# Attention and feed-forward on one core: the first batch's last four down-projection blocks in three rounded passes

## The chip, the cores and the metric

One core of a Trainium2 chip runs the whole program. The metric is the device time of one execution in microseconds (us); lower is better. TensorE (PE) multiplies matrices, and PEld in the profile is its weight load. VectorE (DVE) and ScalarE (ACT) do the elementwise work, GpSimd (POOL) helps them, and SyncE (SP) issues most transfers.

## What is computed

```
# q, k, v: [8 batches, 8 heads, 576, 64];  p: [8, 8, 32, 64];  float32
packed = softmax(p k^T / 8) v                 # per head, 32 rows
attn   = softmax(q packed^T / 8) packed       # per head, 576 rows
x = attn as [8*576, 512]
h = x @ w_in                                  # 512 -> 2048
g = h * tanh(softplus(h))                     # "mish"
out = g @ w_out                               # 2048 -> 512
```

The two weights arrive as 64-bit floats and are turned into float32 on the chip.

## The kernel before

**Work and steps.** The eight batches follow each other, and each has 16 blocks of 128 hidden columns, so there are 128 blocks, and a loop over `t` (L1043) takes one block per step; `f` is the block within its batch. In a step PE does the up-projection of block `t` (`up`, L795: 12 matmuls into two PSUM tiles `ps_h`), ACT applies mish (`mish`, L824) and PE does the down-projection of an earlier block (`down`, L857: four chunks of 128 rows, into four accumulators `acc`). Up to step 16 the block that is brought down is the one of the step before; later it is the one two steps back. The order of a step on PE is: down chunks 0 and 1, up, chunks 2 and 3, with other work let in between.

**Two ways to multiply.** A full float32 matmul appears in the trace as two PE instructions. The other way splits both operands into a rounded high part and a remainder and does three matmuls, high by high, high by remainder and remainder by high (`down_one`, L841). The up-projection does this from block 4 on, the down-projection from batch 1 on. The down-projection of all 16 blocks of batch 0 uses full float32 (L863). For the three passes the weight `wo[f]` is split by `split_wo` (L111: ACT writes `wo_hi`, DVE writes `wo_lo`), which stands in steps 16 to 31, and the activations `g` are split by `halves` (L833).

**Weights of the first batch.** While batch 0 runs, 32 pieces of weight are fetched into eight staging slots `w_st` and decoded: `words` (L685) is two ACT instructions (the second writes `wround`) and two on POOL (the second writes `wsign`), and `join` (L698) is two on DVE for each piece, one with `wsign`, one with `wround`. At odd `f`, `packed_half` (L743) makes the next two blocks' up weights: 16 matmuls on PE into two tiles `ps_w`, then ACT writes `wp_hi` and DVE writes `wp_lo`. The tiles `ps_w`, `ps_a` (turned weights), `ps_pp` (values), `ps_ppT` and `ps_s` (scores) all share one pool of two PSUM buffers, so a tile waits until the one two places before it has been read.

**The next batch's attention.** The attention of batch 1 is a generator (`attention`, L581) that is moved on by one piece at each `advance(gen)` (L907, which first emits what is in `pending`). In steps with even `f` there are three such places, at odd `f` ("chunk" steps) one.

**What sets the order.** PE follows program order throughout. Up to step 16 (`by_hand`) so do DVE, ACT, POOL and SP: each engine takes its instructions in the order in which the code emits them. After that a scheduler orders all engines but PE.

**Memory.** The staging pool `stg` is closed at step 14, and a pool `late` takes its place, with room for the split parts of the first eight weights, three pairs of split activations `g_hi`, `g_lo`, and one pair `r_hi`, `r_lo` for the left-over rows.

Of the kernel before, what the change touches and what calls it, by code (L numbers as in the profile page):

```python
# [17 lines left out]
GB = 3  # L18
# [13 lines left out]
HALFWAY = 8  # L32
SPLIT0 = 14
# [10 lines left out]
def body(  # L44
# [57 lines left out]
    stage = ExitStack()  # L102
    stg = stage.enter_context(tc.tile_pool(name="stg", bufs=STB, side="right"))
    late = []
# [3 lines left out]
    def wo_slot(dtype, name):  # L108
        return wts.tile([P, DO], dtype, name=name, tag="wo", bufs=NF + 1)

    def split_wo(i):  # L111
        if i < HALFWAY:
            wo_hi[i], wo_lo[i] = [late[0].tile([P, DO], F32R, name=f"wo_{x}{i}") for x in ("hi", "lo")]
        else:
            wo_hi[i], wo_lo[i] = wo_slot(F32R, "wo_hi"), wo_slot(F32R, "wo_lo")
        both = [
            nc.scalar.copy(out=wo_hi[i], in_=wo[i]),
            nc.vector.tensor_tensor(out=wo_lo[i], in0=wo[i], in1=wo_hi[i].bitcast(F32), op=ALU.subtract),
        ]
        for x in both:  # L120
            tc.keep_in_program_order(x)
# [255 lines left out]
    class Later(Batch):  # L377
# [203 lines left out]
        def attention(self):  # L581
# [88 lines left out]
    class Weight:  # L670
# [6 lines left out]
        def fetch(self):  # L677
            self.st = stg.tile([P, 2 * FC], I32, name="w_st")
            nc.sync.dma_start(
                out=self.st.rearrange("p (m x) -> p m x", m=2),  # L680
                in_=w_in_v[:, 2 * self.g:2 * self.g + 2, self.n * FC:(self.n + 1) * FC],
            )
            self.dst = wi[self.n // 2][self.g][:, self.n % 2].rearrange("p m x -> p (m x)")

        def words(self):  # L685
            x = self.st.rearrange("p (n t) -> p n t", t=2)
# [20 lines left out]
    class WeightOut(Weight):  # L707
# [3 lines left out]
        def fetch(self):  # L711
            self.st = stg.tile([P, 2 * FC], I32, name="w_st")
            nc.sync.dma_start(out=self.st, in_=w_out_v[:, self.i, :])
            self.dst = wo[self.i] = wo_slot(F32, "wo32")
# [53 lines left out]

    def split_tiles(name="g", bufs=GB):
        return [late[0].tile([P, MAIN], F32R, name=f"{name}_{n}", bufs=bufs) for n in ("hi", "lo")]  # L770

    def split(*srcs):

        hi, lo = split_tiles("r", 1)
# [6 lines left out]
    class Group:  # L781
# [75 lines left out]
    def down(grp, c):  # L857
# [4 lines left out]
        if b == 0:  # L862
# [13 lines left out]
    def down_rest(grp):  # L876
# [6 lines left out]
        if i == 0:  # L883
            rest["o"] = late[0].tile([P, DO], F32, name="o_rest", bufs=1)
# [81 lines left out]
    def fetch(n):  # L966
        for x in pieces[done["fetch"]:n]:
            x.fetch()
# [17 lines left out]
    with tc.manual_schedule(engines={mybir.EngineType.PE}):  # L986
# [56 lines left out]
        for t in range(n_groups + LAG):  # L1043
# [32 lines left out]
            if t == SPLIT0:  # L1076
                stage.close()
                late.append(ctx.enter_context(tc.tile_pool(name="late", bufs=1, side="right", reuse_waits="tile")))
            if 0 <= t - NF < NF:
                split_wo(t - NF)  # L1080
# [43 lines left out]
            if chunk and t > 1:  # L1124
# [28 lines left out]
            if grp:  # L1153
                grp.halves()
                if t <= 13 and t != 1:
                    words(2 * t + 9)
# [6 lines left out]
            if dn and not away:  # L1163
                down(dn, 3)
            if grp and f % 4 == 2 and (b or f == NF - 2):
# [8 lines left out]
            elif b == 0 and not chunk:  # L1174
# [30 lines left out]
```

## Time and profile before

| | us |
|---|---|
| median of 3 runs | 729.82 (729.26 to 731.15) |
| the profiled execution's own time | 729.15 |
| its span, first to last instruction | 726.9 |
| PE busy | 716.2 (99%) |
| DVE / ACT / POOL busy | 430.4 / 315.6 / 70.8 |

The span is what the engines' records cover; 2.25 us of the execution's own time lie around it. "Busy" is an average over stages, so what an engine has to spare is to be read stage by stage. The chain of waits follows the work that ended last back from the end; a stretch in which it runs through PE alone is one in which PE sets the time.

### The profile page before, as it was taken

To read this page: it belongs to the slowest core of one execution; us is meant where nothing else is said; L and a number is where in the kernel's file an instruction comes from. 1 tells how busy PE (TensorE), PEld (TensorE's weight loads), DVE (VectorE), ACT (ScalarE), POOL (GpSimd) and SP (SyncE) were. 2 spreads that over 40 slices of the span, in tenths; PEclk is the share of its full clock that TensorE was granted. 3 is DMA by queue.
4 is the path that set the end of the run, shared out by engine and by line. 5 is a ranking of instruction groups with operands and counts; after the bars stand their busy time and mean duration, and the time that the engine had idled before them with its cause. 6 is when DMAs were issued, how large, how long until landed. Compare 5 with 4: busy or idle time off the path is not lost.

```text
span 726.9 us, 12741 instructions
## 1 busy us (share of the span) xinstructions
PE 716.2 (99%) x5094; PEld 554.9 (76%) x5094; DVE 430.4 (59%) x763; ACT 315.6 (43%) x710; POOL 70.8 (10%) x103
## 2 busy tenths in 40 slices
PE   8899999999999999999999999999999999999997
PEld 5455555788887788787887888887888878888885
DVE  4999878847746466545645566465574566443322
ACT  4876646545533344344342444253442524433221
POOL 0585540000000000000000000000000000000000
PEclk9999999999999999999999999999999999999999
DMA  9999971642203612145102442144101000010002
GB/s 237 303 298 226 311 122 31 130 78 67 33 29 73 110 34 33 66 67 99 18 15 81 67 98 34 44 72 74 33 1 59 15 1 1 1 59 1 1 0 73
DMA packets 187114, 56.34 MB, mean 78 GB/s; under 512 B 175024, under 2 KB 177328, under 8 KB 187056
## 3 DMA queue, kind: packets, MB, share of 16 engines
q1 hardware_dynamic: 183376, 47.14, 29.3%
q0 software_dynamic: 1344, 4.20, 1.5%
q10 hardware_dynamic: 2336, 4.20, 1.5%
q8 instruction: 40, 0.66, 0.4%
q14 instruction: 18, 0.15, 0.1%
HBM read 46.07 MB, written 9.44 MB: 76 GB/s over the span
## 4 chain that ended last, share of the span: by engine, by line
PE 93%; DVE 4%; DMA 1%; SPq 0%; issue 0%; ACT 0%; DVEq 0%
PE ps_h L805 27%; PE acc L843 15%; PE acc L845 14%; PE acc L844 14%; PE acc L863 6%; PE ps_w L719 4%; PE ps_rest L843 2%; PE ps_rest L845 2%; PE ps_rest L844 2%; PE ps_h L467 2%; DMA q_t<-in_q_dram 1%; PE ps_h L540 1%; PE ps_s L467 1%; PE ps_a L520 1%; DVE wi L705 1%; DVE wi L700 1%
## 5 line engine op out<-in xcount | busy, mean ns | idle before, releaser
L827 ACT ACTIVATE g<-ps_h 128x256 f32<-128x256 f32 (+2 forms) x256 | 97.9, 385 | 262.9 <-PE ps_h L805 239.0
L843 PE MATMUL acc<-wo_hi,g_hi 128*128 128x512 f32 x448 | 179.6, 401 | 0.0
L844 PE MATMUL acc<-wo_lo,g_hi 128*128 128x512 f32 x448 | 176.7, 394 | 0.0
L845 PE MATMUL acc<-wo_hi,g_lo 128*128 128x512 f32 x448 | 176.6, 394 | 0.0
L805 PE MATMUL ps_h<-aT_hi,wp_hi 128*128 128x256 f32 x496 | 153.0, 308 | 0.0
L805 PE MATMUL ps_h<-aT_lo,wp_hi 128*128 128x256 f32 x496 | 146.4, 295 | 0.2 <-DVE aT_lo L344 0.2
L805 PE MATMUL ps_h<-aT_hi,wp_lo 128*128 128x256 f32 x496 | 146.2, 295 | 0.0
L838 DVE CAST g_hi<-g 128x512 fp32r<-128x512 f32 x112 | 47.4, 424 | 165.9 <-ACT g L827 165.9
L843 PEld LDWEIGHTS acc<-wo_hi,g_hi 128*128 128x128 f32 x448 | 84.2, 188 | 32.3 <-issue 14.7
L805 PEld LDWEIGHTS ps_h<-aT_hi,wp_hi 128*128 128x128 f32 x496 | 93.4, 188 | 15.2 <-issue 5.9
L805 PEld LDWEIGHTS ps_h<-aT_lo,wp_hi 128*128 128x128 f32 x496 | 93.4, 188 | 12.5 <-issue 3.3
L845 PEld LDWEIGHTS acc<-wo_hi,g_lo 128*128 128x128 f32 x448 | 84.1, 188 | 19.8
L805 PEld LDWEIGHTS ps_h<-aT_hi,wp_lo 128*128 128x128 f32 x496 | 93.4, 188 | 0.0
L844 PEld LDWEIGHTS acc<-wo_lo,g_hi 128*128 128x128 f32 x448 | 84.1, 188 | 9.2
L839 DVE TENSOR_TENSOR g_lo<-g,g_hi 128x512 fp32r<-128x512 f32 x112 | 77.0, 687 | 6.8 <-DVE g_hi L838 0.5
L863 PE MATMUL acc<-wo,g 128*128 128x512 f32 x128 | 61.3, 604 | 0.0
L730 ACT CAST wp_hi<-ps_w 128x512 fp32r<-128x512 f32 x56 | 30.1, 591 | 65.5 <-PE ps_w L719 65.5
L731 DVE TENSOR_TENSOR wp_lo<-ps_w,wp_hi 128x512 fp32r<-128x512 f32 x56 | 35.9, 683 | 9.1 <-ACT wp_hi L730 9.1
L863 PEld LDWEIGHTS acc<-wo,g 128*128 128x128 f32 x128 | 22.4, 189 | 22.7 <-issue 19.2
L872 POOL DMA_DIRECT2D out_dram<-o x16 | 9.0, 561 | 311.2 <-DVE o L852 307.1
L719 PE MATMUL ps_w<-wi,ppT 64*32 64x512 f32 (+1 forms) x576 | 36.8, 548 | 1.9 <-DVE wi L705 1.3
L311 DVE TENSOR_REDUCE sm<-a 128x18 f32<-128x576 f32 (+1 forms) x15 | 11.9, 792 | 28.4 <-ACT a L306 28.4
(135 smaller groups left out, 792.3 us busy)
## 6 DMA issues: line engine op xcount, KB each, us to landing
w_st<-in_moe_w_in_dram SPq DMA_DIRECT2D x16, 512.0 KB, 7.6
w_st<-in_moe_w_out_dram SPq DMA_DIRECT2D x16, 512.0 KB, 7.3
q_n<-in_q_dram SPq DMA_DIRECT2D x56, 144.0 KB, 3.2
v_n<-in_v_dram SPq DMA_DIRECT2D x56, 128.0 KB, 2.8
k_n<-in_k_dram SPq DMA_DIRECT2D x32, 144.0 KB, 3.3
out_dram<-o ACTq DMA_DIRECT2D x14, 256.0 KB, 2.0
k_n<-in_k_dram SPq DMA_DIRECT2D x96, 32.0 KB, 2.0
out_dram<-o POOLq DMA_DIRECT2D x12, 256.0 KB, 2.6
```

The lines of the kernel that those rows point to most:

```text
L467: nc.tensor.matmul(out=ps[u][h * NP:(h + 1) * NP, :], lhsT=packT[u * D:(u + 1) * D, n:n + NP], rhs=xT[u * D:(u + 1) * D, h ^ g, :], start= ...
L719: nc.tensor.matmul(out=ps[h * NP:(h + 1) * NP, :], lhsT=ppTb[row:row + D, g, h * NP:(h + 1) * NP], rhs=w[row:row + D], start=True, stop=Tr ...
L730: nc.scalar.copy(out=hi, in_=ps)
L731: nc.vector.tensor_tensor(out=lo, in0=ps, in1=hi.bitcast(F32), op=ALU.subtract)
L805: nc.tensor.matmul(out=ps, lhsT=w[:, fs], rhs=a[:, g, cs], start=(n == 0), stop=(n == 5))
L827: nc.scalar.activation(out=self.act[:, a:a + m], in_=ps[:, :m], func=AF.Mish)
L838: nc.vector.tensor_copy(out=hi, in_=self.act)
L839: nc.vector.tensor_tensor(out=lo, in0=self.act, in1=hi.bitcast(F32), op=ALU.subtract)
L843: nc.tensor.matmul(out=acc, lhsT=hi[:, cs], rhs=wh, start=start, stop=False)
L844: nc.tensor.matmul(out=acc, lhsT=hi[:, cs], rhs=wl, start=False, stop=False)
L845: nc.tensor.matmul(out=acc, lhsT=lo[:, cs], rhs=wh, start=False, stop=stop)
L863: nc.tensor.matmul(out=accs[c], lhsT=grp.act[:, cs], rhs=wo[f], start=f == 0, stop=f == NF - 1)
```

## The change

- In batch 0, blocks 12 to 15 (`THREE = 12`) are brought down in three rounded passes. `halves` for these blocks (ACT copies the high part, DVE subtracts) comes right after the block's up-projection, and `split_wo` of weights 12 to 15 moves to the ends of steps 11 to 14. In steps 28 to 31 nothing is split any more.
- The staging pool stays open to the end. Its slots hold, once a weight piece is decoded, the split weights 12 to 15 and 0 to 3 and the split activations of blocks 12 to 15; the tiles `wround` and `wsign` (four buffers each) hold the later blocks' `g_hi`, `g_lo` and the left-over rows' `r_hi`, `r_lo`, which had three and one.
- Decoding runs one or two pieces earlier from step 9 on.
- The attention of batch 1 gets a second and third place to move on in odd steps from `f` = 7 (`not chunk or f >= 7`), the maximum of its second softmax is taken for each half on its own, and the division goes from DVE to POOL.

```diff
+THREE = 12
+FIRST_SLOTS = 2
...
     def split_wo(i):
-        if i < HALFWAY:
-            wo_hi[i], wo_lo[i] = [late[0].tile([P, DO], F32R, name=f"wo_{x}{i}") for x in ("hi", "lo")]
+        own = STB - (NF - THREE)
+        if i >= THREE or i < own:
+            pair = slot(F32R, "wo_pair", KEPT <= i < own)
+            wo_hi[i], wo_lo[i] = pair[:, 0], pair[:, 1]
         else:
-            wo_hi[i], wo_lo[i] = wo_slot(F32R, "wo_hi"), wo_slot(F32R, "wo_lo")
+            late = i < own + (NF - THREE) // 2
+            wo_hi[i], wo_lo[i] = wo_slot(F32R, "wo_hi", late), wo_slot(F32R, "wo_lo", late)
...
                 flush()
+                self.peak(slice(g, g + 1))
                 yield
             both = slice(0, 2)
-            self.peak(both)
-            yield
             self.rise(both)
             yield
-            self.share(both)
+            yield
+            self.tally(both)
+            for u in range(2):
+                self.divide(both, u, nc.gpsimd)
+            yield
+            yield
...
         def halves(self):
             if self.b == 0:
-                return
-            self.g = split_tiles()
-            hi, lo = self.g
-            nc.vector.tensor_copy(out=hi, in_=self.act)
+                if self.f < THREE:
+                    return
+                pair = slot(F32R, "g_pair", True)
+                hi, lo = self.g = pair[:, 0], pair[:, 1]
+                nc.scalar.copy(out=hi, in_=self.act)
+            else:
+                hi, lo = self.g = split_tiles()
+                nc.vector.tensor_copy(out=hi, in_=self.act)
             nc.vector.tensor_tensor(out=lo, in0=self.act, in1=hi.bitcast(F32), op=ALU.subtract)
...
-        if b == 0:
+        if b == 0 and f < THREE:
             nc.tensor.matmul(out=accs[c], lhsT=grp.act[:, cs], rhs=wo[f], start=f == 0, stop=f == NF - 1)
...
-            if 0 <= t - NF < NF:
+            if 0 <= t - NF < THREE:
                 split_wo(t - NF)
...
             if t <= 13:
-                join(2 * t + 5 + t // 12 - (t == 9))
+                join(2 * t + 5 + 2 * (t > 9))
...
                 grp.up(0)
                 grp.up(1)
+                if t < NF:
+                    grp.halves()
...
                     if t == 9:
-                        join(2 * t + 5)
+                        join(2 * t + 7)
...
-                    words(2 * t + 9)
+                    words(2 * t + 9 + 2 * (t > 8))
...
+            if THREE <= t + 1 < NF:
+                split_wo(t + 1)
...
-            elif b == 0 and not chunk:
+            elif b == 0 and (not chunk or f >= 7):
                 advance(gen)
```

**PE, steps 7 and 8.** `ps_w` are the up weights made in step 7, `acc` are down chunks, and `ps_a` are the turned attention weights of batch 1. Before:

```order
L719 MATMUL ps_w_919<-wi_1_97,ppT 32x256
L863 MATMUL acc_549<-wo_561,g 128x512
L863 MATMUL acc_550<-wo_561,g 128x512
L863 MATMUL acc_547<-wo_641,g 128x512
L520 MATMUL ps_a_954<-ident,a_693 128x128 x4
L863 MATMUL acc_548<-wo_641,g 128x512
```

Now:

```order
L881 MATMUL acc_549<-wo_561,g 128x512
L881 MATMUL acc_550<-wo_561,g 128x512
L527 MATMUL ps_a_951<-ident,a_693 128x128 x4
L881 MATMUL acc_547<-wo_641,g 128x512
L527 MATMUL ps_a_960<-ident,a_693 128x128 x4
L881 MATMUL acc_548<-wo_641,g 128x512
```

The first `ps_a` stands two down chunks behind `ps_w` where it stood three behind.

**PE, steps 9 and 10.** `ps_pp` is one half of the values' product, `ps_ppT` turns both normalized halves, and `ps_s` are the second scores. Before (12 `up` rows stand where the dots are):

```order
L863 MATMUL acc_549<-wo_644,g 128x512
L556 MATMUL ps_pp<-v_n,a1T_n 32x64 x20
L863 MATMUL acc_550<-wo_644,g 128x512
L863 MATMUL acc_547<-wo_780,g 128x512
L556 MATMUL ps_pp<-v_n,a1T_n 32x64 x20
L863 MATMUL acc_548<-wo_780,g 128x512
...
L863 MATMUL acc_549<-wo_780,g 128x512
L567 MATMUL ps_ppT<-ident,pp 128x128 x2
```

Now:

```order
L881 MATMUL acc_549<-wo_644,g 128x512
L563 MATMUL ps_pp<-v_n,a1T_n 32x64 x20
L881 MATMUL acc_550<-wo_644,g 128x512
L574 MATMUL ps_ppT<-ident,pp 128x128 x2
L881 MATMUL acc_547<-wo_780,g 128x512
L474 MATMUL ps_s_1143<-xT,ppT 32x288 x4
L474 MATMUL ps_s_1144<-xT,ppT 32x288 x4
```

Between the second `ps_pp` and `ps_ppT` there is one down chunk now; there were two chunks and an up-projection. On DVE the same place reads, now:

```order
L763 TENSOR_TENSOR wp_lo<-ps_w_1062,wp_hi 128x256
L763 TENSOR_TENSOR wp_lo<-ps_w_1063,wp_hi 128x256
L711 SCALAR_TENSOR_TENSOR wi_0_98<-wi_0_98,wsign 128x512
L711 SCALAR_TENSOR_TENSOR wi_1_99<-wi_1_99,wsign 128x512
L716 ISA wi_0_98<-wi_0_98,wround 128x1024
L716 ISA wi_1_99<-wi_1_99,wround 128x1024
L276 TENSOR_SCALAR pp<-ps_pp,rs 128x128
L575 COPY ppT<-ps_ppT 128x128 x2
```

The four join rows of a pair of pieces stand between `wp_lo` of step 9 and the normalization `pp` that `ps_ppT` reads, as they did before.

**ACT, steps 11 to 12.** `wo_pair` is the split weight 12, `a_1142` the second softmax of batch 1, `g` the mish of block 12 and `g_pair` its split. Now:

```order
L762 CAST wp_hi<-ps_w_1227 128x256
L699 ACTIVATE wo_1084<-w_st 128x512
L700 ACTIVATE wround<-w_st 128x512
L123 CAST wo_pair<-wo_901 128x512
L313 ACT_TABLE_LOAD
L313 ACTIVATE a_1142<-a_1142 128x1152
L841 ACT_TABLE_LOAD
L841 ACTIVATE g<-ps_h_90 128x256
L841 ACTIVATE g<-ps_h_91 128x256
L843 ACTIVATE g_rest_1268<-ps_h_91 128x64
L853 CAST g_pair<-g 128x512
```

Before, the exponential stood one round of `wp_hi` later, in step 13, and no split followed the mish:

```order
L751 CAST wp_hi<-ps_w_1327 128x256
L306 ACT_TABLE_LOAD
L306 ACTIVATE a_1160<-a_1160 128x1152
L777 CAST r_hi<-g_rest_462 128x4x64
L827 ACT_TABLE_LOAD
L827 ACTIVATE g<-ps_h_90 128x256
```

## Rows read from the trace of the kernel before

**Rows 1.** Windows: length; busy PE, PEld, DVE, ACT, POOL; granted clock; DMA share; GB/s.

```profile
100.00:110.00 10.00, 10.00 (x69) 5.74 (x68) 9.42 (x13) 4.15 (x12) 4.78 (x7) 1.00 0.92 163
200.00:300.00 100.00, 100.00 (x713) 82.82 (x712) 55.38 (x100) 39.49 (x91) 2.82 (x6) 1.00 0.26 54
```

**Rows 2.** Chain of waits, steps 7 to 9: start, length, engine, tile, line, count.

```profile
71.91 2.77 PE acc L863 x6
74.68 0.55 PE ps_a L520 x4
...
83.37 0.59 PE ps_w L719 x16
83.96 1.05 PE acc L863 x2
85.02 0.83 PE ps_pp L556 x40
```

**Rows 3.** Chain of waits, steps 12 to 14.

```profile
103.99 3.43 PE acc L863 x8
107.42 1.59 PE ps_h L805 x12
109.01 0.59 PE ps_w L719 x16
109.61 3.63 PE acc L863 x8
...
114.83 1.72 PE acc L863 x4
```

**Rows 4.** Timeline of PE, batch 1: first of six rounded passes, and what follows them.

```profile
140.18 0.40 PE L843 MATMUL acc<-wo_hi,g_hi 128*128 128x512 f32 x1
...
141.57 0.28 PE L805 MATMUL ps_h<-aT_hi,wp_hi 128*128 128x256 f32 x1
```

**Rows 5.** Timeline of the weight loads, step 8; in brackets idle time and releaser.

```profile
74.57 0.42 PEld L520 LDWEIGHTS ps_a<-ident,a 128*128 128x128 f32 x4 [0.72 <-DVE wp_lo L752]
```

**Rows 6.** Timeline of DVE, steps 5, 9 and 10.

```profile
62.40 1.28 DVE L700 SCALAR_TENSOR_TENSOR wi<-wi,wsign 128x512 int32<-128x512 int32 x2
63.60 1.29 DVE L705 CUSTOM_DVE_ANT_0 wi<-wi,wround 128x1024 uint16<-128x1024 uint16 x2
...
84.46 0.75 DVE L752 TENSOR_TENSOR wp_lo<-ps_w,wp_hi 128x256 fp32r<-128x256 f32 x2 [1.33 <-ACT wp_hi L751]
...
87.01 1.85 DVE L700 SCALAR_TENSOR_TENSOR wi<-wi,wsign 128x512 int32<-128x512 int32 x2
88.78 1.69 DVE L705 CUSTOM_DVE_ANT_0 wi<-wi,wround 128x1024 uint16<-128x1024 uint16 x2
90.39 0.34 DVE L269 TENSOR_SCALAR pp<-ps_pp,rs 128x128 f32<-128x128 f32 x1
```

**Rows 7.** One kind of join instruction: least, median, greatest ns, and when.

```profile
L705 DVE CUSTOM_DVE_ANT_0 wi<-wi,wround x16: 677/880/1098, 19.9 to 102.9; 128x1024 uint16<-128x1024 uint16 x16
```

**Rows 8.** Timeline of ACT, steps 12, 13 and 16.

```profile
104.41 0.67 ACT L688 ACTIVATE wo<-w_st 128x512 f32<-128x512 f32 x1
104.97 0.68 ACT L689 ACTIVATE wround<-w_st 128x512 int32<-128x512 uint32 x1
...
110.36 1.28 ACT L306 ACT_TABLE_LOAD   x1
111.65 1.16 ACT L306 ACTIVATE a<-a 128x1152 f32<-128x1152 f32 x1
...
121.26 0.67 ACT L827 ACTIVATE g<-ps_h 128x256 f32<-128x256 f32 x2
...
121.90 0.65 ACT L117 CAST wo_hi<-wo 128x512 fp32r<-128x512 f32 x1
```

**Rows 9.** Timeline of DVE, steps 16 and 17.

```profile
122.58 0.69 DVE L118 TENSOR_TENSOR wo_lo<-wo,wo_hi 128x512 fp32r<-128x512 f32 x1 [0.18 <-ACT wo_hi L117]
...
127.09 0.69 DVE L839 TENSOR_TENSOR g_lo<-g,g_hi 128x512 fp32r<-128x512 f32 x1
127.85 0.69 DVE L852 COPY o<-acc 128x512 f32<-128x512 f32 x1
```

More of the change, by code (lines that the diff above doesn't have):

```diff
@@ L17 @@
 LAG = 2
-GB = 3
 KVB = 8
@@ L101, in body, with slot, wo_slot @@
     wi = [[const.tile([P, 2, 2, QC], F32, name=f"wi{c}_{g}") for g in range(2)] for c in range(DF // FC)]
[L102 to L104 removed]
+    stg = ctx.enter_context(tc.tile_pool(name="stg", bufs=1, side="right"))
+    KEPT = STB - FIRST_SLOTS - (NF - THREE)
     wo, wo_hi, wo_lo = {}, {}, {}
[L108 to L109 removed]
+    def slot(dtype, name, first):
+        tag, n = ("st_a", FIRST_SLOTS) if first else ("st_b", STB - FIRST_SLOTS)
+        return stg.tile([P, 2, FC], dtype, name=name, tag=tag, bufs=n)
+    def wo_slot(dtype, name, late):
+        tag, n = ("wo_b", NF - THREE) if late else ("wo_a", THREE + 1)
+        return wts.tile([P, DO], dtype, name=name, tag=tag, bufs=n)
     def split_wo(i):
[L112 to L115 removed]
+        own = STB - (NF - THREE)
+        if i >= THREE or i < own:
+            pair = slot(F32R, "wo_pair", KEPT <= i < own)
+            wo_hi[i], wo_lo[i] = pair[:, 0], pair[:, 1]
+        else:
+            late = i < own + (NF - THREE) // 2
+            wo_hi[i], wo_lo[i] = wo_slot(F32R, "wo_hi", late), wo_slot(F32R, "wo_lo", late)
         both = [
@@ L119, in split_wo @@
         ]
-        for x in both:
-            tc.keep_in_program_order(x)
+        if i < THREE:
+            for x in both:
+                tc.keep_in_program_order(x)
     w_in_v = w_in.bitcast(I32).rearrange("(m p) f -> p m f", p=P)
@@ L675, in __init__, with fetch @@
             self.n, self.g = n, g
-        def fetch(self):
-            self.st = stg.tile([P, 2 * FC], I32, name="w_st")
+        def fetch(self, first):
+            self.st = slot(I32, "w_st", first)
             nc.sync.dma_start(
-                out=self.st.rearrange("p (m x) -> p m x", m=2),
+                out=self.st,
                 in_=w_in_v[:, 2 * self.g:2 * self.g + 2, self.n * FC:(self.n + 1) * FC],
@@ L709, in __init__, with fetch @@
             self.i = i
[L711 to L714, printed above, removed]
+        def fetch(self, first):
+            self.st = slot(I32, "w_st", first)
+            nc.sync.dma_start(out=self.st.rearrange("p m x -> p (m x)"), in_=w_out_v[:, self.i, :])
+            self.dst = wo[self.i] = wo_slot(F32, "wo32", self.i >= THREE)
     def weave(b, ps, w, g, h):
@@ L767, in body, with split_tiles @@
     whole = {}
-    def split_tiles(name="g", bufs=GB):
-        return [late[0].tile([P, MAIN], F32R, name=f"{name}_{n}", bufs=bufs) for n in ("hi", "lo")]
+    def split_tiles(name="g"):
+        return [
+            stg.tile([P, MAIN], F32R, name=f"{name}_{n}", tag=tag, bufs=WB)
+            for n, tag in (("hi", "wround"), ("lo", "wsign"))
+        ]
     def split(*srcs):
-        hi, lo = split_tiles("r", 1)
+        hi, lo = split_tiles("r")
         for n, src in enumerate(srcs):
@@ L883, in down_rest @@
         if i == 0:
-            rest["o"] = late[0].tile([P, DO], F32, name="o_rest", bufs=1)
+            rest["o"] = stg.tile([P, DO], F32, name="o_rest", bufs=1)
             nc.scalar.copy(out=rest["o"], in_=ps)
@@ L966, in fetch @@
     def fetch(n):
-        for x in pieces[done["fetch"]:n]:
-            x.fetch()
+        for i, x in enumerate(pieces[:n]):
+            if i >= done["fetch"]:
+                x.fetch(i % STB < FIRST_SLOTS)
         done["fetch"] = max(done["fetch"], min(n, len(pieces)))
```

10 lines of the change are left out of this document (3 added, 7 removed).

## The prediction

> **What bounds the kernel now.** I read the windows first, to see which engine is full in the stretch that the diff touches; then the chain of waits, for PE's order and prices; then the timelines of DVE and ACT in steps 7 to 17, against the new order. In the windows PE is busy for all of 100 to 110 us and of 200 to 300 us at granted clock 1.00, which is the 2.4 GHz level [rows 1]. The chain of waits runs through PE piece by piece in steps 7 to 14 [rows 2, 3]. So from about 60 us to the tail PE sets the time: a shorter PE instruction is a gain one for one, and any gap that opens in PE's queue is a loss one for one, since PE takes its instructions in program order and nothing later has slack to give back. DVE was busy for 9.42 of the 10 us in 100 to 110 [rows 1]; it is the engine on which new waits would form.
>
> All sums are against the profiled execution, 729.15 us (span 726.9 plus 2.25 around it), 0.67 below the median of 729.82. I add the differences to the median.
>
> **What the rounded passes give.** Eight full-float32 instructions, four chunks, take 3.43 us: 0.857 a chunk [rows 3]. Six rounded passes, two chunks, go from 140.18 to 141.57: 1.39 us, 0.695 a chunk [rows 4]. Sixteen chunks change, so PE gets 16 x (0.857 - 0.695) = 2.6 us shorter. Neighbours don't alter that: the extra behind a group of `ps_w` matmuls (3.63 instead of 3.43, [rows 3]) is paid for either kind.
>
> The Trainium skill has a count for this (FP8 and Floating Point Precision, TensorE Precision Notes): a true float32 matmul is four passes through the array. Three rounded passes would then cost three quarters of 0.857 and the gain would be 16 x 0.214 = 3.4 us. The rows show 0.695, not 0.643, so the measured 2.6 stands; 3.4 is a rival below.
>
> **What the moved attention costs: step 7 to 8.** The first `ps_a` needs the PSUM buffer of the older `ps_w`, so it waits for DVE's first `wp_lo`, which waits for ACT's `wp_hi`, behind an exponential with its two table loads. Nothing ahead of these on ACT or DVE changes. Before, the wait was just met: the weight load started at 74.57, released by `wp_lo` [rows 5], while PE was still in its three chunks [rows 2]. Now two chunks stand ahead, PE is there one chunk earlier, and it stands still for 0.86 us. Bounds 0.75 to 0.95, since the old position had no measurable slack.
>
> **Step 9.** `ps_ppT` needs both normalizations `pp`. The second is behind four join instructions on DVE, which are behind `wp_lo`. Count from the end W of `ps_w`.
> - PE: a chunk 1.05, `ps_pp` 0.83, a chunk 1.05 [rows 2]: at `ps_ppT` at W + 2.93, some 0.1 less by the instruction's start, W + 2.85.
> - DVE: before, W was 83.96 and `wp_lo` ran from 84.46 for 0.75 [rows 2, 6], so it ends at W + 1.25 and the joins start at W + 1.2. Four joins with POOL working beside took from 87.01 until the normalization's start at 90.39: 3.38 us [rows 6]. Normalization 0.34 and some 0.1 to the start on PE: W + 5.0.
>
> PE waits 2.15 us. Without POOL beside them the four joins took 62.40 to 64.89, 2.49 [rows 6]; then the wait is about 1.2. At the greatest duration of a join, 1.098 [rows 7], four overlapping by some 0.08 are 4.1, and the wait is 2.85. I take 2.15: ACT decodes four more pieces in step 9, so POOL has work in just that stretch. Before, two chunks and an up-projection (1.72 + 1.59, [rows 3]) lay between, and the same joins were hidden.
>
> **Steps 11 to 13.** The exponential of the second softmax now stands before the mish of block 12, whose split PE wants first. From the end E of step 11's `ps_w`:
> - PE: four chunks 3.63, up 1.59, two chunks 1.72 [rows 3]: wants `g_pair` high at E + 6.9.
> - ACT: `wp_hi` done at E + 0.75 (110.36 against 109.60, [rows 3, 8]); the last `words`, 104.41 to 105.65, 1.24; the split of weight 12, 0.6; table load 1.28; exponential 1.16; table load 1.28 again, back to mish; then from mish to the end of a cast behind it 1.29 (121.26 to 122.55) [all rows 8]. Sum E + 7.6. The table loads are two either way; now they lie in front of an operand that PE waits for.
>
> Hence 0.7 us for the high part. DVE's remainder takes 0.69 more [rows 9], while PE has two passes (0.46, [rows 4]) to do with the high part: 0.3 with the hand-over. Together 1.0; bounds 0.6 (the second load or the split overlapping more than I count) to 1.6 (DVE's maximum, behind its own joins, reaching ACT later).
>
> **The rest.** Blocks 13 to 15: the remainder is ready within 0.1 us of PE's need in steps 14 and 16; I take 0.1, bounds 0 to 0.3. In steps 16 to 18 DVE has from `wo_lo` to the next `g_lo` 4.51 us (122.58 to 127.09), and a copy of 0.69 moves in front of `g_lo` [rows 9]: 5.9 to the end of `g_lo`, starting some 1.85 after the end of step 15's up. PE wants it 7.8 after that (eight chunks at 0.695, less one, two ups, two passes). That is even; 0.1, bounds 0 to 0.5.
>
> At nothing: POOL's two division instructions (POOL idle after its last decoding piece, and the result is wanted two steps on); the splits moved from steps 28 to 31 (DVE had 55.38 busy of 100 us there, [rows 1], and PE never waited); the four shared buffers of `wround` and `wsign` (a split pair is read two steps after it is written, and four buffers, one of them lent to the left-over rows for a step, still give back the oldest in time; if not, PE would wait in each odd batch, some tenths every fourth block); SP's queue, which keeps its order.
>
> **Sum.** -2.6 + 0.86 + 2.15 + 1.0 + 0.1 + 0.1 = +1.6 us: 731.4. With all low bounds (0.75 + 1.2 + 0.6) the net is -0.05, 729.8; with all high ones (0.95 + 2.85 + 1.6 + 0.3 + 0.5 = 6.2) it is +3.6, 733.4.
>
> **Rivals.**
> 1. *The gain comes whole.* The waits of steps 7, 9 and 12 don't form, because an earlier slip of PE gives DVE and ACT time that I count twice, or the buffers are handed over earlier than the order says. -2.6: 727.2. For it: PE never waited in these steps before. Against: step 8's wait needs no estimate, as its releaser's time is in the trace. Chance 0.11.
> 2. *The joins at full length.* With POOL busy through all four, each join goes towards 1.098 [rows 7], and step 9's wait to 2.85; ACT's chain slips by as much as its DVE inputs do, 1.5. -2.6 + 0.9 + 2.85 + 1.5 + 0.2 = +2.8: 732.6, slower. It decides from where a join averages 1.0 us. For it: 87.01 and 88.78 show 0.93 and 0.85 with POOL only partly busy [rows 6]. Against: only single instructions reached 1.1. Chance, with the upper part of my own bounds, 0.35.
> 3. *Step 9's wait is small.* If POOL is done early, it is 1.2, and step 12's 0.6: net about 0, 729.8. Within my range; part of the 0.54 below.
> 4. *Four passes against three.* With rounded passes at 0.643 a chunk, 3.4 - 4.2: +0.8, 730.6. The rows speak against it; 0.03, within the 0.54.
>
> **How the numbers follow.** About 0.3% (2.2 us) is what a measurement of this kernel tells from no change. My likeliest is +1.6, 731.4, within that band; below 727.6 only rival 1 lies, above 732.0 rival 2. Forecast with rivals 3 and 4: 0.54. The range for 8 in 10 cuts most of rival 1 and the last of rival 2: 729.0 to 733.2.
>
> **What would show it.** In the profile after: 48 rounded passes in batch 0 (16 chunks by 3) where 32 full-float32 instructions stood, some 0.23 us apart; PE idle before `ps_a` in step 8 released by `wp_lo`, about 0.9; before `ps_ppT` in step 10's beginning released by `pp`, about 2; before the first pass with `g_pair` in step 13 released by ACT, about 1. No other idle time of PE before the tail, and a granted clock of 1.00. I am wrong if PE has no idle time there, or if a wait stands in batches 1 to 7, where the shared buffers are.

## The result, and the profile after

The changed kernel takes 733.94 us (median of 6 runs, 732.68 to 734.45) where the kernel before takes 729.34 beside it (6 runs, 729.12 to 731.15). The ratio is 1.0056, 95% interval 1.0043 to 1.0069: slower by 4.6 us (3.1 to 5.0), and above the range of the prediction, which ended at 733.2. The profiled execution took 733.94 us, its span is 732.0.

I read the windows first, as in [rows 1]. Columns as there.

```profile
70.00:80.00 10.00, 9.38 (x60) 5.91 (x59) 8.00 (x11) 8.36 (x17) 3.99 (x5) 1.00 1.01 379
80.00:90.00 10.00, 8.83 (x119) 4.58 (x118) 8.49 (x14) 7.29 (x16) 5.76 (x7) 1.00 0.85 230
90.00:100.00 10.00, 9.01 (x55) 4.36 (x56) 8.00 (x14) 4.70 (x10) 6.09 (x9) 0.83 0.44 69
100.00:110.00 10.00, 10.00 (x56) 5.92 (x54) 8.71 (x14) 7.21 (x13) 3.00 (x4) 1.00 0.96 166
110.00:120.00 10.00, 8.65 (x57) 6.11 (x55) 8.67 (x12) 4.74 (x14) 3.25 (x3) 1.00 0.06 14
...
150.00:160.00 10.00, 9.53 (x55) 8.03 (x54) 3.59 (x8) 6.10 (x14) 0.00 (x0) 1.00 0.51 81
```

Two of the same stretches before:

```profile
90.00:100.00 10.00, 10.00 (x69) 5.59 (x68) 6.40 (x14) 6.04 (x15) 3.15 (x5) 1.00 0.43 69
110.00:120.00 10.00, 10.00 (x50) 5.22 (x49) 7.06 (x11) 6.16 (x11) 0.00 (x0) 1.00 0.01 2
```

Before, PE was busy for all of each of the six stretches at granted clock 1.00. Now it stands still in five of them, and in 90 to 100 us its clock is 0.83. What it waited for between 55 and 170 us (total, times, longest):

```profile
PE ps_ppT L574 <- DVE pp L276: 2.2, 1, 2.2
PE acc L863 <- DVE g_pair L857: 0.7, 1, 0.7
PE ps_w L730 <- DVE a L494: 0.6, 1, 0.6
PE ps_a L527 <- DVE wp_lo L763: 0.6, 1, 0.6
PE acc L861 <- ACT g_pair L853: 0.6, 1, 0.6
PE ps_h L519 <- ACT g L841: 0.5, 1, 0.5
```

The third row stands in the kernel before too, between 50 and 60 us. The others are new. I call these waits flagged, since the profile itself shows them as idle time in front of an instruction; not every loss is flagged. Where the time goes is read by laying the starts of the up-projections beside those of before, block by block. This table holds that for the profiled executions of all kernels told of below: start in that kernel minus start in the kernel before, in us, with the difference at block 6 (under 0.8) taken off, since the change begins behind it.

```
kernel            block 12   block 19   block 24   block 126
changed kernel      4.70       4.50       5.19       5.23
e1_rounded_only     1.94       5.16       5.86       5.98
e2_no_rounding      3.11       3.10       3.10       3.08
e3_joins_later      0.92       6.18       6.87       6.92
e4_filled_wait      3.13       2.90       3.59       3.71
e5_divide_on_dve    4.71       4.16       4.86       4.89
e6_own_r            3.18       2.97       3.00       2.69
e7_new_cadence     -0.11       3.10       3.79       3.83
e8_new_cadence_r   -0.10       5.06       5.09       4.78
e9_joins_behind    -0.11       3.33       3.36       3.04
e10_two_blocks     -0.10       4.05       4.08       4.11
e11_order          -0.10      -0.01       0.02      -0.24
e12_in_turn        -0.11      -0.83      -0.80      -1.11
```

In the changed kernel all of the loss arises up to block 24; the hundred blocks behind it add nothing. Up to block 12, where only the attention and the decoding differ, 4.70 us are lost. From there to block 19, where the rounded passes stand, 0.20 are won: the passes are 2.6 shorter by the sum of the prediction, so 2.4 are lost beside them. Then 0.69 are lost.

**Up to block 12.** PE in steps 9 and 10:

```profile
86.76 0.90 PE L563 MATMUL ps_pp<-v_n,a1T_n 128*32 128x64 f32 x40
...
88.56 0.27 PE L574 MATMUL ps_ppT<-ident,pp 128*128 128x128 f32 x1
90.99 0.33 PE L574 MATMUL ps_ppT<-ident,pp 128*128 128x128 f32 x1 [2.16 <-DVE pp L276]
...
92.11 1.21 PE L474 MATMUL ps_s<-xT,ppT 64*32 64x288 f32 x16
93.25 2.07 PE L881 MATMUL acc<-wo,g 128*128 128x512 f32 x2
```

And DVE there:

```profile
86.27 0.76 DVE L763 TENSOR_TENSOR wp_lo<-ps_w,wp_hi 128x256 fp32r<-128x256 f32 x2 [0.76 <-ACT wp_hi L762]
86.94 1.69 DVE L711 SCALAR_TENSOR_TENSOR wi<-wi,wsign 128x512 int32<-128x512 int32 x2
88.56 2.11 DVE L716 CUSTOM_DVE_ANT_0 wi<-wi,wround 128x1024 uint16<-128x1024 uint16 x2
90.59 0.34 DVE L276 TENSOR_SCALAR pp<-ps_pp,rs 128x128 f32<-128x128 f32 x1
```

The normalization stands behind four joins, 86.94 to 90.59 = 3.65 us where I had 3.38 from [rows 6], and PE waits 2.16 (in brackets: idle time, and what ended it). Behind the wait the 16 score matmuls take 1.21 us (0.71 in e2, below, behind the same wait) and a pair of chunks 2.07 (1.12 there): for a part of the window the clock is at its lower level, 1.2 GHz.

**Blocks 12 to 19.** PE's first rounded pass, and the one that waits in step 14:

```profile
111.06 0.50 PE L861 MATMUL acc<-wo_pair,g_pair 128*128 128x512 f32 x1 [0.60 <-ACT g_pair L853]
111.40 0.40 PE L862 MATMUL acc<-wo_pair,g_pair 128*128 128x512 f32 x1
111.79 0.50 PE L863 MATMUL acc<-wo_pair,g_pair 128*128 128x512 f32 x1
...
117.95 0.50 PE L863 MATMUL acc<-wo_pair,g_pair 128*128 128x512 f32 x1 [0.74 <-DVE g_pair L857]
```

DVE ahead of the second:

```profile
114.09 1.64 DVE L711 SCALAR_TENSOR_TENSOR wo<-wo,wsign 128x512 int32<-128x512 int32 x1
115.76 1.53 DVE L716 CUSTOM_DVE_ANT_0 wo<-wo,wround 128x1024 uint16<-128x1024 uint16 x1
117.22 0.68 DVE L857 TENSOR_TENSOR g_pair<-g,g_pair 128x512 fp32r<-128x512 f32 x1
```

POOL at the same time:

```profile
113.81 2.94 POOL L327 TENSOR_TENSOR a<-a,sm 128x576 f32<-128x576 f32 x2 [7.10 <-PE ps_h L819]
```

At 62.40 us before, two joins of a kind took 1.28 us together [rows 6]; here, beside POOL's division, one takes 1.64 and one 1.53. e5, below, takes the division away.

**Behind block 19.** ACT at 151 to 153 us:

```profile
151.26 0.39 ACT L841 ACTIVATE g<-ps_h 128x256 f32<-128x256 f32 x1
...
151.65 0.71 ACT L791 CAST r_hi<-g_rest 128x256 fp32r<-128x256 f32 x2
152.25 0.63 ACT L123 CAST wo_hi<-wo 128x512 fp32r<-128x512 f32 x1
152.77 0.39 ACT L841 ACTIVATE g<-ps_h 128x256 f32<-128x256 f32 x1
```

Two casts of left-over rows and one of a weight stand ahead of a mish that PE waits for (0.47, the last row of the waits).

### The profile page after: what moved, and what is told of

Read it like the earlier page. It is cut to its first block, busy times and chain, and to the rows that moved or that the text cites. A ratio compares the mean times of both kernels' runs of the same rounds, so it can differ in the third digit from the quotient of the medians.

```text
span 732.0 us, 12793 instructions
## 1 busy us (share of the span) xinstructions
PE 717.0 (98%) x5110; PEld 558.4 (76%) x5110; DVE 434.7 (59%) x768; ACT 315.7 (43%) x714; POOL 74.2 (10%) x105
## 4 chain that ended last, share of the span: by engine, by line
PE 89%; ACT 4%; DVE 4%; DMA 1%; issue 1%; SPq 0%; DVEq 0%; ACTq 0%
PE ps_h L819 26%; PE acc L861 15%; PE acc L863 14%; PE acc L862 14%; PE ps_w L730 4%; PE acc L881 3%; PE ps_rest L861 2%; PE ps_rest L863 2%; PE ps_rest L862 2%; PE ps_h L474 2%; DMA q_n<-in_q_dram 1%; PE ps_h L547 1%; PE ps_s L474 1%; PE ps_a L527 1%; DVE wi L716 1%
## 5 line engine op out<-in xcount | busy, mean ns | idle before, releaser
L861 PE MATMUL acc<-wo_hi,g_hi 128*128 128x512 f32 x224 | 90.3, 403 | 0.0
L861 PE MATMUL acc<-wo_pair,g_hi 128*128 128x512 f32 x224 | 89.0, 397 | 0.0
L862 PE MATMUL acc<-wo_lo,g_hi 128*128 128x512 f32 x224 | 88.4, 395 | 0.0
L863 PE MATMUL acc<-wo_hi,g_lo 128*128 128x512 f32 x224 | 88.3, 394 | 0.0
L863 PE MATMUL acc<-wo_pair,g_lo 128*128 128x512 f32 x224 | 88.3, 394 | 0.0
L862 PE MATMUL acc<-wo_pair,g_hi 128*128 128x512 f32 x224 | 88.0, 393 | 0.0
L861 PEld LDWEIGHTS acc<-wo_hi,g_hi 128*128 128x128 f32 x224 | 42.1, 188 | 20.8 <-issue 10.9
L861 PEld LDWEIGHTS acc<-wo_pair,g_hi 128*128 128x128 f32 x224 | 42.1, 188 | 11.2 <-issue 3.8
L863 PEld LDWEIGHTS acc<-wo_hi,g_lo 128*128 128x128 f32 x224 | 42.1, 188 | 9.9
L863 PEld LDWEIGHTS acc<-wo_pair,g_lo 128*128 128x128 f32 x224 | 42.0, 188 | 9.7
L881 PE MATMUL acc<-wo,g 128*128 128x512 f32 x96 | 47.5, 616 | 0.0
L862 PEld LDWEIGHTS acc<-wo_pair,g_hi 128*128 128x128 f32 x224 | 42.1, 188 | 4.9
```

The source lines that it names most:

```text
L861: nc.tensor.matmul(out=acc, lhsT=hi[:, cs], rhs=wh, start=start, stop=False)
L862: nc.tensor.matmul(out=acc, lhsT=hi[:, cs], rhs=wl, start=False, stop=False)
L863: nc.tensor.matmul(out=acc, lhsT=lo[:, cs], rhs=wh, start=False, stop=stop)
L881: nc.tensor.matmul(out=accs[c], lhsT=grp.act[:, cs], rhs=wo[f], start=f == 0, stop=f == NF - 1)
```

## Experiments

The first four set the two halves of the change against each other, and take the wait of step 9 apart. Theory A was that the denser attention makes the loss. Edits are against the changed kernel where nothing else is said, and dots mark what is left out.

**e1_rounded_only**, the attention as before, the rest as changed:

```diff
-                self.peak(slice(g, g + 1))
...
-            self.rise(both)
-            yield
-            yield
-            self.tally(both)
-            for u in range(2):
-                self.divide(both, u, nc.gpsimd)
+            self.peak(both)
             yield
+            self.rise(both)
             yield
+            self.share(both)
...
-            elif b == 0 and (not chunk or f >= 7):
+            elif b == 0 and not chunk:
```

> The rounded passes, the early decoding and the reused staging slots stay; the second batch's attention goes back to its steps of before. Theory A (the loss comes from the waits and the lower clock that the denser attention makes in steps 7 to 10 and 14, the rounded passes give 2.6 us): no wait on the second ps_ppT in step 9, no stretch under a granted clock of 0.98 between 60 and 130 us, and the time at or below the kernel before, 727 to 730 us; up to 2.4 us of the gain may go to a late operand in block 16, since the splits put 4.8 us of DVE work into steps 11 to 16. Rival B (the splits on ACT and DVE and the reused slots are what costs): 732 to 735 us, near the changed kernel.

Measured: 735.08 us (ratio 1.0071, 1.0051 to 1.0092). Theory A as I had it fell. 1.94 are lost up to block 12 (1.25 flagged in front of `ps_ppT`, since the joins are early here too), and 3.2 more up to block 19 instead of a gain. DVE in step 14:

```profile
116.12 1.35 DVE L318 TENSOR_REDUCE sm<-a 128x36 f32<-128x1152 f32 x1
...
118.13 1.36 DVE L327 TENSOR_TENSOR a<-a,sm 128x1152 f32<-128x1152 f32 x1
119.53 0.78 DVE L345 STREAM_TRANSPOSE at<-a 128x576 f32<-128x576 f32 x1
120.23 0.65 DVE L853 TENSOR_TENSOR g_pair<-g,g_pair 128x512 fp32r<-128x512 f32 x1
```

The old attention puts the whole second softmax in front of block 14's remainder, which PE reads one step later and waits 1.15 for. Full float32 has no remainder, so before this order cost nothing. A step later block 15's high part is late as well, by 1.68, behind casts of the attention and of the up weights on ACT, and behind that wait the clock falls: it is 0.90 in 120 to 130 us and 0.93 in 130 to 140. So a part of the 3.2 is the clock.

**e2_no_rounding**, the kernel before with the changed attention and decoding: the reverse of the edit above, and, against the kernel before,

```diff
-                join(2 * t + 5 + t // 12 - (t == 9))
+                join(2 * t + 5 + 2 * (t > 9))
...
-                        join(2 * t + 5)
+                        join(2 * t + 7)
...
-                    words(2 * t + 9)
+                    words(2 * t + 9 + 2 * (t > 8))
```

> The other half alone: the kernel before, with only the denser attention of the second batch and the early decoding of the changed kernel; the down-projections stay full float32. Theory A: the waits of steps 8 and 9 and the low clock behind them stand here too, 0.8 + 2.3 + 1.6 us, and the waits of step 14 in part: the span 4 to 6 us longer than before, 733 to 736 us. Rival B: within 1 us of the kernel before, 728.5 to 730.5 us.

Measured: 733.78 us (1.0057, 1.0042 to 1.0072). All of it is lost up to block 12, 3.11 us in the profile, with the same wait of 2.16. The profiled execution took 732.13 us, its mean clock was 0.999, and the window behind the wait is at 1.00:

```profile
90.00:100.00 10.00, 8.89 (x60) 4.53 (x61) 9.71 (x16) 4.83 (x10) 7.59 (x10) 1.00 0.55 88
```

The three other executions took 733.74 to 733.96 us at mean clocks of 0.996 and 0.997. So each half alone loses about as much as both together or more (5.8 and 4.5 us against 4.6): the denser attention makes the wait of step 8 and, with the joins that stand there, that of step 9, but it also takes the softmax out of the way of the splits. That the joins have their part in step 9 is seen on both sides: e1 has a wait there without the denser attention, and e3, below, has none with it.

**e3_joins_later**, the changed kernel without the earlier decoding, and without the join behind step 9's up weights, which the kernel before has too (its piece is joined earlier in the step):

```diff
-                join(2 * t + 5 + 2 * (t > 9))
+                join(2 * t + 5 + t // 12)
...
-                    if t == 9:
-                        join(2 * t + 7)
...
-                    words(2 * t + 9 + 2 * (t > 8))
+                    words(2 * t + 9)
```

> The changed kernel with the joins and the decoding pieces of steps 9 to 13 put back to the step in which they stood before, so that in step 9 the second normalization stands directly behind wp_lo on DVE, not behind four joins. Theory A: the second ps_ppT no longer waits (under 0.3 us), the granted clock of 90 to 100 us is 0.98 or more, and 3.9 us of the loss is gone: about 730.0 us (729 to 731). Rival C (the clock falls whatever PE waits for there, or the joins only make another wait): 732 us or more, with the clock of 90 to 100 us still under 0.9.

Measured: 735.87 us (1.0091, 1.0076 to 1.0106). Theory A held for step 9: its wait is gone, the clock of 90 to 100 us is 1.00, and 0.92 is lost at block 12. It failed for the time: waits of 1.8 and 3.5 us came in steps 13 and 14, and behind the second the clock is 0.84 in 120 to 130 us. The last piece's decoding now stands behind the division on POOL:

```profile
111.76 2.95 POOL L327 TENSOR_TENSOR a<-a,sm 128x576 f32<-128x576 f32 x2 [6.57 <-PE ps_h L819]
114.79 0.62 POOL L701 TENSOR_SCALAR wo<-wo 128x512 f32<-128x512 f32 x1
115.49 0.62 POOL L705 TENSOR_SCALAR wsign<-wo 128x512 f32<-128x512 f32 x1
```

DVE waits for it with its join, and block 13's remainder is behind that:

```profile
116.14 0.69 DVE L711 SCALAR_TENSOR_TENSOR wo<-wo,wsign 128x512 int32<-128x512 int32 x1 [2.46 <-POOL wsign L705]
116.75 1.28 DVE L716 CUSTOM_DVE_ANT_0 wo<-wo,wround 128x1024 uint16<-128x1024 uint16 x2
117.96 0.68 DVE L857 TENSOR_TENSOR g_pair<-g,g_pair 128x512 fp32r<-128x512 f32 x1
```

**e4_filled_wait**, the changed kernel with dummy matmuls in the wait:

```diff
             elif b == 0 and (not chunk or f >= 7):
+                if t == 9:
+                    warm(10)
                 advance(gen)
```

> The changed kernel with ten extra matmuls of zeros put on PE ahead of the second ps_ppT of step 9, some 2.1 us long, into a PSUM buffer that nobody reads then: PE is late for its operand by as much as before, but it is busy while it waits. Theory A (the idle time itself costs 2.3 us and the clock that falls behind it costs 1.6 us more): the granted clock of 90 to 100 us is 0.98 or more, the up-projection of block 10 starts 1.6 us earlier than in the changed kernel, and the time is about 732.3 us (731.6 to 733). Rival D (the low clock there costs nothing, or it falls in any case): 733.5 to 734.5 us.

Measured: 732.84 us (1.0050, 1.0035 to 1.0065), all four executions between 732.57 and 733.23, 1.1 below the changed kernel:

```profile
90.00:100.00 10.00, 9.99 (x64) 4.86 (x62) 9.80 (x16) 5.01 (x10) 7.60 (x10) 1.00 0.55 87
```

The operand comes as late as before, PE is busy until then, and the clock stays at 1.00: block 12 is at 3.13, not 4.70. With e2 and e6 (3.11 and 3.18 with the wait, clock 1.00) against the changed kernel and e5 (4.70 and 4.71, clock 0.83) the fall costs 1.6 us where it comes. It doesn't come in every execution: five of the changed kernel's six have a mean clock of 0.996 or 0.997, and e4's four have 0.998 to 1.000. Why the medians are 1.1 apart and not 1.6 is not shown.

**e5_divide_on_dve**, the division moved whole from POOL to DVE:

```diff
-            for u in range(2):
-                self.divide(both, u, nc.gpsimd)
+            self.divide(both)
```

> The changed kernel with the division of the second softmax as one VectorE instruction (1.36 us) instead of two on POOL (2.95 us). Theory A (POOL's division stretches the two DVE joins beside it from about 0.68 us each to 1.6 and 1.5, and that makes the remainder of block 13's split late in step 14): the two joins take 0.7 us each, g_pair's remainder comes 1.8 - 1.36 = about 0.45 us earlier, and the wait of 0.74 us before its pass falls to 0.3 us; 733.5 us. Rival (POOL's work costs DVE nothing): the joins stay at 1.5 us or more, the wait grows by 1.36 us to about 2.1, 735.3 us.

Measured: 733.62 us (1.0049, 1.0037 to 1.0062), and the flagged wait is 0.4:

```profile
115.65 0.68 DVE L710 SCALAR_TENSOR_TENSOR wo<-wo,wsign 128x512 int32<-128x512 int32 x1
116.37 0.69 DVE L715 CUSTOM_DVE_ANT_0 wo<-wo,wround 128x1024 uint16<-128x1024 uint16 x1
```

The two joins take 1.37 us together where they took 3.17 beside POOL's division. So the division, 2.95 us on POOL, had cost DVE 1.8; on DVE itself it costs 1.36. From block 12 to 19 the kernel wins 0.55 where the changed kernel won 0.20, so 0.35 by the move.

**e6_own_r**: of the four buffers of `wround` and of `wsign`, one each is kept apart for the left-over rows (one of the places is shown):

```diff
-        hi, lo = split_tiles("r")
+        hi, lo = split_tiles("r", "_r")
```

> The changed kernel with the split tiles of the left-over rows in buffers of their own, as before (the same memory: three buffers of wround and wsign for the blocks, one of each for the left-over rows). Theory A (sharing the four buffers lets the scheduler put two casts of left-over rows and a weight cast ahead of the mish of block 21, which makes ps_h wait in 152 to 154 us): in the order the casts stand apart again as before, the wait of 0.47 us on g in front of ps_h at 153 us is gone, and blocks from 22 on start 0.7 us earlier than in the changed kernel: 733.2 us. Rival (the wait there is the batch's own, or the order of casts is nothing): 733.9 us and the wait stays.

Measured: 732.01 us (1.0037, 1.0024 to 1.0051). The wait at 153 us is gone; from block 19 to 24 it loses 0.03 and not 0.69:

```profile
90.00:100.00 10.00, 9.02 (x61) 4.67 (x62) 9.70 (x16) 4.69 (x10) 7.60 (x10) 1.00 0.41 66
...
150.00:160.00 10.00, 10.00 (x57) 8.61 (x57) 4.87 (x9) 4.51 (x13) 0.00 (x0) 1.00 0.42 66
```

Behind block 24 it wins another 0.3 (2.69 at block 126). e8, e9, e11 and e12, which have the same buffers, do so too; e10, which has them as well, does not, and what makes it was not looked for. The rest of the 1.9 between the medians goes with the clock, as far as can be told: the five executions took 731.35 to 733.35 us, at mean clocks from 1.000 down to 0.997.

The remaining six look for an order in which the passes pay.

**e7_new_cadence** and **e8_new_cadence_r** (the second also with the buffers of e6):

```diff
             self.tally(both)
-            for u in range(2):
-                self.divide(both, u, nc.gpsimd)
-            yield
+            self.divide(both)
             yield
...
-                join(2 * t + 5 + 2 * (t > 9))
+                join(2 * t + 5 - (t == 9) + (t > 10) + (t > 11))
...
-                        join(2 * t + 7)
+                        join(2 * t + 5)
...
-                    words(2 * t + 9 + 2 * (t > 8))
+                    words(2 * t + 9)
...
-            elif b == 0 and (not chunk or f >= 7):
+            elif b == 0 and (not chunk or f >= 11):
```

> Rounded passes as in the changed kernel, with the second batch's attention, the joins and the decoding as in the kernel before up to step 10; from step 11 on one further place for the attention at the end of odd steps, the maximum taken in two parts, the exponential in step 12 behind the cast of block 12's split, the division whole on VectorE in step 13, and joins one or two pieces earlier in steps 11 and 12. Theory A (the gain of 2.6 us is there and each wait is one of place: steps 8 and 9 as before have none, the exponential behind the cast of an even step delays no operand, the division on POOL is gone): no wait over 0.4 us between 60 and 130 us, granted clock 1.00 there, about 728 us with the 0.7 us at 153 us still in it (727.3 to 729.3). Rival (DVE and ACT have no room for the splits of four blocks in steps 12 to 15, wherever the attention stands): waits of 2 us or more on g_pair, wp_lo or aT_lo in 105 to 130 us, 730 us or more.

> The kernel with the new places of the attention and, beside it, buffers of their own for the split tiles of the left-over rows. Theory A: 0.7 us below the one without that, about 727.3 us (726.6 to 728.6), which is faster than both kernels by 0.3% or more. Rival (no room for the splits): 729.3 us or more, and the same 0.7 us between the two.

Measured: 733.65 us (1.0052, 1.0039 to 1.0065) and 733.28 (1.0049, 1.0036 to 1.0062). Up to block 12 nothing is lost, as expected. From block 19 to 24 the first loses 0.69 and the second 0.03, as e6 said. But between blocks 12 and 19 there are waits of 2.9 and 1.5 us (2.7 and 1.0 in e8, whose clock is 0.76 in 110 to 120 us, behind the first). So in both the rival came true. DVE in step 12 of e7, where block 12's high part was ready at 104.8:

```profile
105.13 1.29 DVE L709 SCALAR_TENSOR_TENSOR wo<-wo,wsign 128x512 int32<-128x512 int32 x2
...
106.94 1.29 DVE L714 CUSTOM_DVE_ANT_0 wo<-wo,wround 128x1024 uint16<-128x1024 uint16 x2
108.14 0.69 DVE L855 TENSOR_TENSOR g_pair<-g,g_pair 128x512 fp32r<-128x512 f32 x1
```

The joins of a step are emitted ahead of its split, so the remainder runs behind six of them.

**e9_joins_behind** is e8 with the joins behind the split from step 12 on; one join each moves into steps 10 and 11 (not shown), the last piece is decoded in step 13, and the attention's cast of `aT_hi` comes one place later:

```diff
                 if t < NF:
                     grp.halves()
+                if THREE <= t < NF:
+                    join(31 + (t > 13))
...
-                    words(2 * t + 9)
+                    words(min(2 * t + 9, 31) + (t > 12))
...
                 self.back(g)
                 yield
+                if g == 0:
+                    yield
                 self.upper(g)
```

> The version with new places and own buffers for the left-over rows, changed where its trace showed waits: from step 12 on the joins stand behind the block's split on VectorE (the remainder of block 12 was ready at 104.84 us and ran at 108.14, behind six joins), one join piece each is moved into steps 10 and 11, the last piece is decoded in step 13 and joined in step 14, and the cast of aT_hi comes one place later, behind the mish of block 14. Theory A (each wait is one of place, and PE's gain of 2.6 us is there to be had): the waits of 2.7 and 1.0 us on g_pair are gone, at most 1.3 us of waits on DVE is left around block 16, and the time is about 728 us (727 to 729.3), at or below the kernel before. Rival (VectorE is simply full in steps 12 to 15, so that what is moved comes back as a wait on another operand): 3 us of waits or more between 100 and 130 us, 730.5 us or more.

Measured: 732.11 us (1.0034, 1.0021 to 1.0047), above its forecast. One new wait is left, with the length that the rival had, and behind it the clock falls (0.83 in 120 to 130 us):

```profile
125.45 0.50 PE L861 MATMUL acc<-wo_pair,g_pair 128*128 128x512 f32 x1 [3.13 <-ACT g_pair L853]
```

**e10_two_blocks** rounds blocks 12 and 13 alone, with the attention and the decoding of before, the buffers of e6 and the joins of steps 12 and 13 behind the split (only the choice of blocks is shown):

```diff
+ROUNDED = (12, 13)
...
-        if b == 0 and f < THREE:
+        if b == 0 and f not in ROUNDED:
```

> Only blocks 12 and 13 of the first batch in three rounded passes, 14 and 15 in full float32 as before, with the attention and the decoding of the kernel before, the joins of steps 12 and 13 behind the block's split, and own buffers for the left-over rows. The gain is 8 x 0.162 = 1.3 us, and the splits before the exponential of step 13 add 2.7 us to VectorE instead of 5.5 us. Theory A: no wait over 0.4 us that the kernel before doesn't have, 728.3 us (727.5 to 729). Rival (no room): waits of 1.5 us or more in steps 12 to 16, 730 us or more.

Measured: 733.22 us (1.0059, 1.0045 to 1.0073), so the forecast of 728.3 missed. The attention's transposes and `wp_lo` are behind the joins on DVE, and PE waits 2.0 in front of `ps_w` and 1.3 for `wp_lo`; the clock is 0.83 in 110 to 120 us, behind the first. Half the rounding in this order costs more than all of it in that of e9.

**e11_order** starts from e9 and clears what stood ahead of its last wait: the last piece is decoded in step 11 and joined in step 12, the last weight's split stands behind `wp_lo`, and the last pieces of the attention come a step later:

```diff
-                if THREE <= t < NF:
-                    join(31 + (t > 13))
+                if t == THREE:
+                    join(32)
...
-                    words(min(2 * t + 9, 31) + (t > 12))
+                    words(2 * t + 9 + (t > 10))
...
-                        finish(gen)
+                        next(gen, None)
...
                     wps[nb, nch] = packed_w(nb, nch)
+                    if nb > b == 0:
+                        split_wo(NF - 1)
```

> The version with the joins behind the splits had no wait left between 60 and 118 us and a single one of 3.13 us at block 15, where the mish stood on ACT behind the second cast of aT_hi and the cast of wp_hi, and these behind VectorE's join and split of the last weight. Here the last piece is decoded in step 11 and joined in step 12, where VectorE had 1.9 us without work; the last weight's split stands behind wp_lo; and the second cast of aT_hi and its remainder come in step 15. All four blocks are rounded. Theory A (the 2.6 us are there, every lost microsecond is a wait of place): at most 0.7 us of waits in 100 to 130 us, granted clock 1.00 there, 727.5 us (726.6 to 728.8), faster than the kernel before. Rival (VectorE and ACT have no room, the wait only moves again): 2 us of waits or more, 730 us or more.

Measured: 728.81 us (0.9991, 0.9982 to 1.0000): level with the kernel before, at the upper end of the forecast. In step 14 PE waits 0.99 for block 13's high part, whose mish ACT had behind this cast:

```profile
109.07 0.62 ACT L123 CAST wo_pair<-wo 128x512 fp32r<-128x512 f32 x1 [1.17 <-DVE wo L716]
109.71 1.28 ACT L841 ACT_TABLE_LOAD   x1
111.00 0.66 ACT L841 ACTIVATE g<-ps_h 128x256 f32<-128x256 f32 x2
```

**e12_in_turn**, e11 with one line more, which joins the weight of block 13 first:

```diff
                 if t == THREE:
+                    join(30)
                     join(32)
```

> The last version with one change: in step 12 the weight of block 13 is joined on VectorE ahead of the two other pieces and not in turn with them, so that its second join ends at about 107.9 us and not at 109.0. ACT's cast of that weight, which the table load and the mish of block 13 stand behind, was waiting for it (idle 1.17 us). Theory A: the wait of 0.99 us in front of block 13's first rounded pass is gone, and so is most of what PE loses around it (that pair and its remainder took 1.5 us longer than six passes); VectorE then makes block 14 or 15 late by up to 0.7 us; 0.8 us below the last version, about 728.0 us (727.4 to 728.8), ratio 0.998. Rival (the next operand is just as late): 728.8 us.

Measured: 728.13 us where the kernel before takes 729.67 beside it, ratio 0.9978 (0.9969 to 0.9987): faster than both kernels, though by 0.2% only (beside e11 the kernel before took 729.21). PE's waits between 60 and 160 us, of which the first stands in the kernel before too:

```profile
PE ps_w L730 <- DVE a L494: 0.6, 1, 0.6
PE acc L863 <- DVE g_pair L857: 0.5, 1, 0.5
```

## Why the prediction was wrong

The mechanism was right in the places that it named, and it stopped at them.

- *The gain.* The profile after has 48 rounded passes in batch 0, and where nothing is late they stand 0.23 us apart, 0.69 to 0.70 a chunk, as sized. Of the 2.6 us e12 brings in 0.72 between blocks 12 and 19; 0.31 of its 1.11 at block 126 arises behind block 24, with the buffers of e6.
- *Steps 8 and 9*, sized 0.86 and 2.15, cost 3.1 together (block 12 in e2, e4 and e6), of which 0.6 and 2.16 are flagged; *step 13*, sized 1.0, cost 1.1. Each had the releaser that was named. (Steps 13 to 16 are read from the starts of the up-projections, less 0.39 us by which a record behind a full-float32 instruction begins early: its first row is 0.68 long and not 0.28.)
- *"A granted clock of 1.00"* failed. I priced the idle time of step 9 at its own length. The clock fell behind it, in most executions to judge by their mean clocks: 1.6 us, shown by e4 and by the profiles in which it did not fall (e2, e6). This is the largest of the terms that I left out.
- *"At nothing: POOL's two division instructions (POOL idle after its last decoding piece)"* failed. POOL was idle, but DVE's two joins beside it took 1.8 us longer, and step 14, within the 0.1 for blocks 13 to 15, cost 1.0 (0.65 in e5, where the division takes DVE's own time). I had read the same effect in [rows 6] for the joins of step 9, 3.38 us with POOL beside them and 2.49 without, and did not ask what POOL's division would stand beside. In e3 the same instructions held up the decoding behind them. By the Trainium skill (SBUF — State Buffer, "SBUF: two separate sides") a VectorE instruction that reads two operands from SBUF and a GpSimd instruction that reads SBUF shut each other out for the whole of an instruction. The rows agree: 1.64 and 1.53 us beside POOL, 0.68 and 0.69 without (e5).
- *"The four shared buffers"* were put at nothing, "if not, PE would wait in each odd batch". It cost 0.69 once, at 153 us, in batch 1, which is where the prediction's last sentence said that a wait would prove it wrong. No row shows a wait for a buffer; with the shared tiles the scheduler put three casts ahead of a mish, and with tiles apart it did not (e6).
- *Behind step 14*, up to block 19, 0.3 were lost, all between the up-projections of blocks 15 and 16, where I had 0.1 for blocks 13 to 15 and 0.1 for steps 16 to 18. The 7.8 us that I gave PE for the latter go with six chunks (6 x 0.695 + 2 x 1.59 + 0.46 = 7.8) and not with eight less one, as the words have it. The attention has one further place in odd steps, at their end, and not two as the text ahead of the prediction says; no number hangs on it.

The losses that I had sized came to 4.2 us and measured 3.1 + 1.1 + 0.3 = 4.5; those that I had at nothing, or as good as nothing, measured 1.6 + 1.0 + 0.7 = 3.3. With the gain of 2.6 that is the +5.2 of the profile, where I had +1.6. Step 13's 1.1 and the 0.3 were read from starts alone; no run takes either away by itself. None of the rivals came true: rival 2 had the step-9 wait at 2.85, and it was 2.16. The fourth spoke of passes at 0.643 a chunk, and they stayed at 0.695.

Why e12 does not bring in all of it is seen in the spacing of its passes: in front of each block's first pass with the remainder there are 0.30 to 0.87 us and not 0.23, of which the idle column flags 0.47 in one place alone. In all four blocks that pass starts 0.05 to 0.06 us behind the end of DVE's remainder (107.11, 112.44, 118.46 and 123.10 us), so the remainder is still late in each. An order in which none is late was not found.

## What to carry to other kernels

Work that moves onto an engine in program order is paid by what is queued behind it, so write down for each late operand the whole queue ahead of it, and put what PE reads next first. The same four blocks in rounded passes made the kernel 4.6 us slower or 1.5 faster; between the two stand the places of the attention, of the joins, casts and table loads, the engine of the division, and buffers kept apart. Price an idle stretch of PE of some 2 us at its length and, as a risk, a fall of the clock besides (here 1.6 us). An idle engine is no free place: 2.95 us of division on idle POOL took 1.8 us from busy DVE.

## What the runs showed of the hardware

- PE's clock behind one and the same wait of 2.16 us fell in some executions and not in others: in the window of 90 to 100 us it is 0.83 in the changed kernel and e5, 1.00 in e2 and e6, 1.6 us apart at block 12. Executions of one kernel differ too, by their mean clocks (e2: 0.999 in one, 0.996 or 0.997 in three). In e7 a wait of 2.94 us passed with the clock at 1.00, and in e10 the clock was 0.83 behind one of 1.97. What decides it was not settled. Dummy matmuls of 2.3 us in the wait kept it at 1.00.
- The idle column understates a late operand between rounded passes: a pass is shown as 0.39 us long where the next one starts 0.23 behind it, so up to 0.16 us of each wait is hidden, and behind a pass that waited the next starts after 0.33 to 0.34.
- A switch of ACT's table and back around one exponential took 1.28 us each, and the activation started 0.01 us behind each load (109.71 + 1.28 against 111.00). The Trainium skill (ScalarE: Activation LUTs, "What ACT_TABLE_LOAD costs") adds 1.38 us of draining to each switch; no such time stands ahead of the loads or behind them here (109.07 + 0.62 against 109.71).
